# Attention with a gated residual: the last group's gates fetched through ScalarE's queue, its final additions on VectorE

## The chip, the cores and the metric

The kernel runs on one core of one Trainium2 chip. The metric is the device time of one execution in microseconds; medians are given, and each comparison uses runs of the kernel before on the same chip. The experiments ran on three chips, on which the kernel before took 938.11, 937.95 and 938.00 us, so differences of some 0.2 us between experiments are not read. A time is about 2 us longer than the span of the profile (first to last instruction): 938.09 against 936.1 us before the change.

Names: TensorE is PE in the profile, its weight loads PEld, VectorE DVE, ScalarE ACT, GpSimd POOL, SyncE SP. A "q" after the name (POOLq) marks a record of that engine's sequencer.

## The reference, cut to what matters

```python
xn = layernorm(x)                                   # x: 2048 x 640, bf16
q  = xn @ wq                                        # 32 heads of 192
p  = softmax(q @ k[last 512].T * 192**-0.5)
s  = (p @ v[last 512]) @ wo                         # 2048 x 640
g  = silu((sigmoid(xn @ w_gate) * (xn @ w_up)) @ w_down)
return x + s * g
```

## The kernel before

The gate `g` is computed first and stored to a scratch tensor `gB_d` in device memory. Attention then runs over 32 blocks: 8 groups of 4 heads (`g`), each over 4 stretches of 512 rows (`s`). A block computes scores and exponentials, then the products with V; in between it does the output projection of the block before (`stage_wo`), whose four tiles of 128 x 640 are added up over the groups in `acc`. Before the last group, GpSimd prepares each accumulator as `acc * gate + x`. The last group then needs one multiplication (projection times gate) and one addition (plus `acc`) per tile, in `finish`.

```python
    fin = ...tile_pool(name="fin", bufs=2)          # t_sb, xa_sb
    fout = ...tile_pool(name="fout", bufs=4)        # o_sb
    gate_pool = ...tile_pool(name="gate_pool", bufs=TQ + 1)     # TQ = 4

    def load_gate(t):
        gB_sb = gate_pool.tile([P, D], BF16, name="gBa_sb")
        nc.gpsimd.dma_start(gB_sb[:], gB_d[t * P:(t + 1) * P, :])
        return gB_sb

    def prep_last(t):                       # in the last group but one
        ...                                 # loads gate and x of tile t + 1 on nc.gpsimd
        nc.gpsimd.tensor_tensor(acc[t][:], acc[t][:], gB_sb[:], ALU.mult)
        nc.gpsimd.tensor_tensor(acc[t][:], acc[t][:], x_sb[:], ALU.add)

    def finish(ps, gB_sb, t, d0, d1, add):
        t_sb = fin.tile([P, D], F32, name="t_sb")
        o_sb = fout.tile([P, D], BF16, name="o_sb")
        d = slice(d0, d1)
        nc.vector.tensor_tensor(t_sb[:, d], ps, gB_sb[:, d], ALU.mult)
        add.tensor_tensor(o_sb[:, d], t_sb[:, d], acc[t][:, d], ALU.add)
        nc.sync.dma_start(of[t * P:(t + 1) * P, d], o_sb[:, d])

    def stage_wo(n, q):
        ...
        if g == NG - 1:
            for tt in range(t, min(t + 4, NST * TQ)):
                if tt not in gates:
                    gates[tt] = load_gate(tt)
            gB_sb = gates[t]
        if n == last and q == TQ - 1:       # the last tile, in two halves
            ps, h = bank2(), D // 2
            for i in range(2):
                wo_mm(ps[:, i, :], n, q, [(i * h, h)], i * h)
                finish(ps[:, i, 0:h], gB_sb, t, i * h, (i + 1) * h, nc.vector)
            return
        ...
        if g == NG - 1:
            finish(oA[:, 0:D], gB_sb, t, 0, D, nc.gpsimd if n >= last - 1 else nc.vector)
```

The softmax here doesn't subtract the row's maximum and nothing guards it: scores larger than these inputs give would overflow.

Of the kernel before, what the change touches and what calls it, by code (L numbers as in the profile page):

```python
# [9 lines left out]
ALU = mybir.AluOpType  # L10
# [5 lines left out]
def kernel(  # L16
# [13 lines left out]
    nc = tc.nc  # L30
    P = 128
# [4 lines left out]
    S, D = xf.shape  # L36
# [10 lines left out]
    NST = S // 512  # L47
    TQ = 4
# [6 lines left out]
    NG = NPAIR // G  # L55
# [18 lines left out]
    def bank2():  # L74
        b = ring.pop(0)
        ring.append(b)
        return ps_all[:, 2 * b:2 * b + 2, :]

    def flat(ps):
        return ps.rearrange("p b n -> p (b n)")  # L80
# [7 lines left out]
    gB_d = dram.tile([S, D], BF16, name="gB_d")  # L88
# [29 lines left out]
    def load_k(hp, eng):  # L118

        k_sb = k_pool.tile([P, KC * PC, 2, HF], BF16, name="k_sb")  # L120
        for i in range(2):
            hk = (2 * hp + i) // rep
            eng.dma_start(
                k_sb[:, :, i, :],
                A_k_cache[0, hk, Sk - W:Sk, :].rearrange("(p k) (j e) -> p (k j) e", k=KC, j=PC),
            )
        k_of[hp] = k_sb

    def load_v(hp, eng):
        v_t[hp] = []  # L130
        for i in range(2):
            hk = (2 * hp + i) // rep
            vt = v_tiles[(2 * hp + i) % NV]
            eng.dma_start(
                vt[:, :, 0:DH],
                A_v_cache[0, hk, Sk - W:Sk, :].rearrange("(p j) d -> p j d", j=KC),
            )
            v_t[hp].append(vt)

    def load_wq(hp, eng):  # L140


        if hp % G == 0:
            wq_t[hp // G] = wq_pool.tile([P, G * PC // 2, NCD * 2, 2, HF], BF16, name="wqp")
        wqp = wq_t[hp // G]
        for j in range(PC):
            jj = (hp % G) * PC + j
            r = HI if jj % 2 else LO
            for i in range(2):
                d0 = (2 * hp + i) * DH + j * HF  # L150
                eng.dma_start(
                    wqp[r, jj // 2, :, i, :],
                    wq_r[:, :, :, d0:d0 + HF].rearrange("p c h n -> p (c h) n"),
                )

    def turn_k(hp):
        kT = kt_pool.tile([P, KC * PC, P], BF16, name="kT")
        nc.sync.dma_start_transpose(kT[:], k_of[hp][:].rearrange("p k i e -> p (k i e)"))
        kT_t[hp] = kT


    with ExitStack() as bctx:
# [147 lines left out]
        for s in range(NST):  # L310
            hT_sb = hpool.tile([P, NF, 512], BF16, name="hT_sb")
            for f in range(NF):
# [13 lines left out]
                if s + 1 < NST:  # L326
                    t = (s + 1) * TQ
# [7 lines left out]
            for q in range(TQ):  # L335
# [8 lines left out]
                gB_sb = bwork.tile([P, D], BF16, name="gB_sb")  # L344
# [3 lines left out]
                t = s * TQ + q  # L348
# [20 lines left out]
    small = ctx.enter_context(tc.tile_pool(name="small", bufs=8))  # L369
    fin = ctx.enter_context(tc.tile_pool(name="fin", bufs=2))  # L370
    fout = ctx.enter_context(tc.tile_pool(name="fout", bufs=4))
    gate_pool = ctx.enter_context(tc.tile_pool(name="gate_pool", bufs=TQ + 1))

    acc = [acc_pool.tile([P, D], F32, name=f"acc{t}") for t in range(NST * TQ)]
    wo_t = {}

    def load_wo(g, eng):
        wo_g = wo_pool.tile([P, G * PC, D], BF16, name="wo_g")
        eng.dma_start(wo_g[:], wo_r[:, g * G * PC:(g + 1) * G * PC, :])
        wo_t[g] = wo_g  # L380

    def load_ahead(g, s):


        if s < G:
            load_wq(g * G + s, nc.scalar)
            load_k(g * G + s, nc.scalar)
        elif s == G:
            for hp in range(g * G, (g + 1) * G):
                load_v(hp, nc.scalar)  # L390
                turn_k(hp)
        if s == NST - 1:
            load_wo(g, nc.scalar)
# [22 lines left out]
    def stage_s(n, pp, c):  # L416

        g, s = blocks[n]
        kT, qT = kT_t[g * G + pp], qT_t[n]
        if c == 0:  # L420
            E_t[n, pp] = e_pool.tile([P, KC, 2, 512], BF16, name="E")
        ps = bank2()
        for j in range(PC):
            for b, r in enumerate((LO, HI)):
                nc.tensor.matmul(  # L425
                    ps[:, b, :], lhsT=kT[r, c * PC + j, :], rhs=qT[r, pp * PC + j, :],
                    start=(j == 0), stop=(j == PC - 1),
                )
        nc.scalar.activation(E_t[n, pp][:, c, :, :], ps, AF.Exp, scale=scale_qk)  # L429
# [24 lines left out]
            nc.sync.dma_start_transpose(oT[:], o_st[:].rearrange("p q d -> p (q d)"))  # L454
            oT_t[n, pp] = oT

    def load_gate(t):
        gB_sb = gate_pool.tile([P, D], BF16, name="gBa_sb")
        nc.gpsimd.dma_start(gB_sb[:], gB_d[t * P:(t + 1) * P, :])  # L459
        return gB_sb  # L460

    prep_in = {}

    def prep_load(t):
        gB_sb = load_gate(t)
        x_sb = fin.tile([P, D], BF16, name="xa_sb")
        nc.gpsimd.dma_start(x_sb[:], xf[t * P:(t + 1) * P, :])
        prep_in[t] = gB_sb, x_sb

    def prep_last(t):  # L470

        if t == 0:
            prep_load(t)
        if t + 1 < NST * TQ:
            prep_load(t + 1)
        gB_sb, x_sb = prep_in[t]
        nc.gpsimd.tensor_tensor(acc[t][:], acc[t][:], gB_sb[:], ALU.mult)  # L477
        nc.gpsimd.tensor_tensor(acc[t][:], acc[t][:], x_sb[:], ALU.add)

    def wo_mm(oA, n, q, d_ch, base=0):  # L480
        g, s = blocks[n]
        nn = G * PC
        for cc in range(nn):
            pp, j = divmod(cc, PC)
            for d0, dsz in d_ch:
                nc.tensor.matmul(  # L486
                    oA[:, d0 - base:d0 - base + dsz], lhsT=oT_t[n, pp][:, q * PC + j, :],
                    rhs=wo_t[g][:, cc, d0:d0 + dsz],
                    start=(cc == 0), stop=(cc == nn - 1),
                )  # L490

    def finish(ps, gB_sb, t, d0, d1, add):
        t_sb = fin.tile([P, D], F32, name="t_sb")
        o_sb = fout.tile([P, D], BF16, name="o_sb")
        d = slice(d0, d1)
        nc.vector.tensor_tensor(t_sb[:, d], ps, gB_sb[:, d], ALU.mult)  # L496
        add.tensor_tensor(o_sb[:, d], t_sb[:, d], acc[t][:, d], ALU.add)  # L497
        nc.sync.dma_start(of[t * P:(t + 1) * P, d], o_sb[:, d])

    gates = {}  # L500

    def stage_wo(n, q):
        g, s = blocks[n]
        t = s * TQ + q
        if g == NG - 1:

            for tt in range(t, min(t + 4, NST * TQ)):
                if tt not in gates:
                    gates[tt] = load_gate(tt)
            gB_sb = gates[t]  # L510
        if n == last and q == TQ - 1:

            ps, h = bank2(), D // 2
            for i in range(2):
                wo_mm(ps[:, i, :], n, q, [(i * h, h)], i * h)
                finish(ps[:, i, 0:h], gB_sb, t, i * h, (i + 1) * h, nc.vector)
            return
        oA = flat(bank2())
        wo_mm(oA, n, q, d_chunks)
        if g == NG - 1:  # L520
            finish(oA[:, 0:D], gB_sb, t, 0, D, nc.gpsimd if n >= last - 1 else nc.vector)
        elif g == 0:
            nc.vector.tensor_copy(acc[t][:], oA[:, 0:D])
        else:
            nc.vector.tensor_tensor(acc[t][:], oA[:, 0:D], acc[t][:], ALU.add)  # L525
        if g == NG - 2:
            prep_last(t)

    blocks = [(g, s) for g in range(NG) for s in range(NST)]
    last = len(blocks) - 1  # L530
# [4 lines left out]
    for n, (g, s) in enumerate(blocks):  # L535

        todo = [(pp, c) for pp in range(G) for c in range(KC)]
        for k, (pp, c) in enumerate(todo):
            stage_s(n, pp, c)
            if k % 2 == 1 and k // 2 < G * PC // 2 and n < last:  # L540
                stage_q(n + 1, k // 2)
        if g + 1 < NG:
            load_ahead(g + 1, s)

        pv = [(n, pp, i) for pp in range(G) for i in range(2)]
        wo = [(n - 1, q) for q in range(TQ)] if n > 0 else []
        if n < last:
            for k, u in enumerate(pv):
                stage_pv(*u)
                if wo:  # L550
                    stage_wo(*wo[k])
        else:
            for k, u in enumerate(pv):
                stage_pv(*u)
                if k == 1:
                    stage_wo(*wo.pop(0))
            for u in wo:
                stage_wo(*u)
# [31 lines left out]
```

## Time and profile before

| | before |
|---|---|
| time, median of 3 runs | 938.09 us (938.05 to 938.12) |
| span of the profile | 936.1 us |
| TensorE busy | 921.1 us |
| TensorE's last matmul ends | 927.73 us |
| VectorE's last addition ends | 930.87 us |
| SyncE's last wait for an output ends | 932.9 us |
| GpSimd's drain ends | 935.32 us |

The page of the kernel before, cut: busy time and share of the span; busy tenths of the 40 slices of the span; and the queue of DMAs that GpSimd issues (packets, MB, share).

```profile
span 936.1 us, 18189 instructions
...
PE 921.1 (98%) x7945; PEld 539.8 (58%) x8025; DVE 446.7 (48%) x636; ACT 303.8 (32%) x340; POOL 106.8 (11%) x130
...
PE   9999999999999999999999999999999999999996
...
DVE  4443532454444444444444444444444444444654
...
POOL 0070000100000000000000000000000006666005
...
q0 software_dynamic: 4368, 14.03, 5.7%
```

TensorE is busy nine tenths or more of every slice but the last. So what can be gained is in the last slice, where GpSimd (POOL) is at work again after a pause. The timeline of the kernel before, from 914 us on, cut; columns are start, length, engine, line, operation, and in brackets the idle time before it and what ended it:

```profile
916.16 11.57 PE L486 MATMUL ps_all<-wo_g,oT 128*128 128x512 bf16 x82
...
926.65 0.82 DVE L496 TENSOR_TENSOR t_sb<-ps_all,gBa_sb 128x640 f32<-128x640 f32 x1 [1.23 <-POOL o_sb L497]
928.07 1.52 POOL L497 TENSOR_TENSOR o_sb<-t_sb,acc_1587 128x640 bf16<-128x640 f32 x1
928.14 0.49 DVE L496 TENSOR_TENSOR t_sb<-ps_all,gBa_sb 128x320 f32<-128x320 f32 x1 [0.66 <-POOL o_sb L497]
928.66 1.28 DVE L497 TENSOR_TENSOR o_sb<-t_sb,acc_1588 128x320 bf16<-128x320 f32 x1
929.87 0.48 DVE L496 TENSOR_TENSOR t_sb<-ps_all,gBa_sb 128x320 f32<-128x320 f32 x1
930.38 0.49 DVE L497 TENSOR_TENSOR o_sb<-t_sb,acc_1588 128x320 bf16<-128x320 f32 x1
```

TensorE ends at 916.16 + 11.57 = 927.73. GpSimd still adds the last full tile until 929.59, and VectorE's product at 928.14 had to wait 0.66 us for GpSimd, because the product buffer `t_sb` has two copies and GpSimd was still reading one. The half addition at 928.66, beside GpSimd's, took 1.28 us; the other took 0.49. In the table of waits of the same stretch (total us, times, longest us):

```profile
DVE t_sb L496 <- POOL o_sb L497: 2.7, 3, 1.2
```

The records of the kernel's closing line are waits and drains of the engines' sequencers. They are listed with count, shortest/median/longest in ns, and first and last start:

```profile
L585 POOLq DRAIN  x3: 40/102/7804, 927.5 to 935.8; - x3
L585 SPq DRAIN  x3: 7/7/13, 932.9 to 935.6; - x3
```

GpSimd's long drain began at 927.5 and took 7.80 us, so it ended at 935.3. SyncE had waited for every output and began its own drain at 932.9. The closing barrier, which takes 0.78 us, starts only after both: its first record comes at 935.37. So GpSimd alone held the end for some 2.3 us.

### The profile page before, as it was taken

What the parts mean: (1) busy time and instruction counts of PE and PEld (TensorE: products, weight loads), DVE (VectorE), ACT (ScalarE), POOL (GpSimd) and SP (SyncE); (2) the same over time, 40 slices, a digit from 0 to 9 for tenths busy, and PEclk for the clock granted to TensorE, in tenths of its full rate; (3) what the DMA queues carried; (4) which work ended last, traced back from release to release, by engine and by line L of the source; (5) the groups of instructions that cost most, each with busy time, mean ns of one, the idle gap of its engine ahead of it and who ended that gap; (6) DMA issues with size and microseconds to landing.
All of it is one profiled execution on the core that took longest, in us unless ns stands there. A gap on an engine that the chain in (4) does not pass through costs nothing.

```text
span 936.1 us, 18189 instructions
## 1 busy us (share of the span) xinstructions
PE 921.1 (98%) x7945; PEld 539.8 (58%) x8025; DVE 446.7 (48%) x636; ACT 303.8 (32%) x340; POOL 106.8 (11%) x130
## 2 busy tenths in 40 slices
PE   9999999999999999999999999999999999999996
PEld 5545445565555565555556555555555556666664
DVE  4443532454444444444444444444444444444654
ACT  4333322433333333333333333333333333333340
POOL 0070000100000000000000000000000006666005
PEclk9999999999999999999999999999999999999999
DMA  9566030376334523463346324632563348553434
GB/s 281 155 124 118 18 95 15 96 115 100 81 62 65 114 73 53 76 112 77 54 71 121 76 48 70 113 65 70 70 106 69 77 73 162 125 133 98 91 84 119
DMA packets 270144, 87.18 MB, mean 93 GB/s; under 512 B 250288, under 2 KB 266736, under 8 KB 270064
## 3 DMA queue, kind: packets, MB, share of 16 engines
q1 hardware_dynamic: 146864, 47.20, 25.8%
q10 hardware_dynamic: 118832, 24.78, 13.9%
q0 software_dynamic: 4368, 14.03, 5.7%
q8 instruction: 63, 1.03, 0.4%
q14 instruction: 17, 0.14, 0.0%
HBM read 44.70 MB, written 5.24 MB: 53 GB/s over the span
## 4 chain that ended last, share of the span: by engine, by line
PE 96%; issue 1%; POOL 1%; DMA 0%; DVE 0%; ACT 0%; SPq 0%; DVEq 0%; ACTq 0%; POOLq 0%
PE ps_all L409 22%; PE ps_all L486 21%; PE ps_all L441 19%; PE ps_all L425 18%; PE ps_all L319 10%; PE ps_all L339 6%; PE ps_all L260 1%; DMA x_sb_138<-in_A_x_dram 0%; POOL o_sb L497 0%; ACT E L429 0%; DVE t_sb L496 0%; POOL gBa_sb L459 0%; DVE stats L222 0%; SPq L175 0%; ACT xnT_93 L275 0%
## 5 line engine op out<-in xcount | busy, mean ns | idle before, releaser
L429 ACT ACTIVATE E<-ps_all 128x1024 bf16<-128x1024 f32 x256 | 247.8, 1022 | 496.2 <-PE ps_all L425 443.7
L486 PE MATMUL ps_all<-wo_g,oT 128*128 128x128 bf16 (+2 forms) x1473 | 224.9, 295 | 3.3
L414 DVE CAST qT<-ps_all 128x1024 bf16<-128x1024 f32 x96 | 117.5, 1224 | 226.4 <-PE ps_all L409 226.4
L425 PE MATMUL ps_all<-qT,kT 64*128 64x512 bf16 x1536 | 186.7, 376 | 0.0
L441 PEld LDWEIGHTS <-E 128*128 128x128 bf16 x2048 | 171.0, 98 | 24.4 <-issue 13.6
L486 PEld LDWEIGHTS <-oT 128*128 128x128 bf16 x1536 | 121.4, 97 | 76.2
L409 PEld LDWEIGHTS <-wqp 64*128 64x128 bf16 x1920 | 93.4, 94 | 113.8 <-issue 0.3
L425 PEld LDWEIGHTS <-kT 64*128 64x128 bf16 x1536 | 72.3, 94 | 91.8 <-issue 8.4
L448 DVE TENSOR_TENSOR o_st<-ps_all,rden 128x768 bf16<-128x768 f32 x128 | 122.5, 957 | 4.8 <-DVE rden L447 0.5
L447 DVE RECIPROCAL rden<-ps_all 128x4 f32<-128x4 f32 x128 | 23.3, 182 | 98.9 <-PE ps_all L441 98.7
L477 POOL TENSOR_TENSOR acc_1573<-acc_1573,gBa_sb 128x640 f32<-128x640 f32 x1 | 1.4, 1397 | 603.4 <-DVE acc_1573 L525 603.4
L325 DVE TENSOR_TENSOR hT_sb<-ps_all,sig_sb 128x512 bf16<-128x512 f32 x48 | 33.1, 691 | 50.9 <-PE ps_all L319 40.9
L409 PE MATMUL ps_all<-xnT_94,wqp 64*128 64x512 bf16 x240 | 55.7, 376 | 0.0
L409 PE MATMUL ps_all<-xnT_95,wqp 64*128 64x512 bf16 x240 | 55.7, 376 | 0.0
L409 PE MATMUL ps_all<-xnT_96,wqp 64*128 64x512 bf16 x240 | 55.7, 376 | 0.0
L409 PE MATMUL ps_all<-xnS_90,wqp 64*128 64x512 bf16 x240 | 55.6, 376 | 0.0
L409 PE MATMUL ps_all<-xnS_91,wqp 64*128 64x512 bf16 x240 | 55.6, 376 | 0.0
L409 PE MATMUL ps_all<-xnS_92,wqp 64*128 64x512 bf16 x240 | 55.6, 376 | 0.0
L409 PE MATMUL ps_all<-xnT_93,wqp 64*128 64x512 bf16 x240 | 55.4, 376 | 0.0
L409 PE MATMUL ps_all<-xnS_89,wqp 64*128 64x512 bf16 x240 | 55.3, 376 | 0.0
L339 PE MATMUL ps_all<-wd_sb,hT_sb 128*128 128x128 bf16 (+1 forms) x377 | 52.4, 298 | 0.4
L324 ACT ACTIVATE sig_sb<-ps_all 128x512 bf16<-128x512 f32 x48 | 28.6, 597 | 56.6 <-PE ps_all L319 56.2
(159 smaller groups left out, 696.5 us busy)
## 6 DMA issues: line engine op xcount, KB each, us to landing
wqp<-in_A_wq_dram ACTq DMA_DIRECT2D x84, 80.0 KB, 3.0
wo_g<-in_A_wo_dram ACTq DMA_DIRECT2D x7, 960.0 KB, 5.1
k_sb<-in_A_k_cache_dram ACTq DMA_DIRECT2D x28, 192.0 KB, 4.6
gBa_sb<-gB_d POOLq DMA_DIRECT2D x32, 160.0 KB, 2.9
gB_d<-gB_sb POOLq DMA_DIRECT2D x16, 160.0 KB, 2.5
xa_sb<-in_A_x_dram POOLq DMA_DIRECT2D x16, 160.0 KB, 3.2
out_dram<-o_sb SPq DMA_DIRECT2D x15, 160.0 KB, 2.2
wd_sb<-in_B_w_down_dram SPq DMA_DIRECT2D x1, 1920.0 KB, 11.8
```

The source lines that it names most:

```text
L319: nc.tensor.matmul(gu[:, i, :], lhsT=w[:, c, f * P:(f + 1) * P], rhs=xnT[s][:, c, :], start=(c == 0), stop=(c == NCD - 1),)
L324: nc.scalar.activation(sig_sb[:], gu[:, 0, :], AF.Sigmoid)
L325: nc.vector.tensor_tensor(hT_sb[:, f, :], gu[:, 1, :], sig_sb[:], ALU.mult)
L339: nc.tensor.matmul(oB_ps[:, d0:d0 + dsz], lhsT=hT_sb[:, f, q * P:(q + 1) * P], rhs=wd_sb[:, f, d0:d0 + dsz], start=(f == 0), stop=(f == NF ...
L409: nc.tensor.matmul(ps[:, b, :], lhsT=wq_t[g][r, u, 2 * c + h].rearrange("p i e -> p (i e)"), rhs=x[s][r, c, :], start=(c == 0 and h == 0), ...
L414: nc.vector.tensor_copy(qT_t[n][:, 2 * u:2 * u + 2, :], ps)
L425: nc.tensor.matmul(ps[:, b, :], lhsT=kT[r, c * PC + j, :], rhs=qT[r, pp * PC + j, :], start=(j == 0), stop=(j == PC - 1),)
L429: nc.scalar.activation(E_t[n, pp][:, c, :, :], ps, AF.Exp, scale=scale_qk)
L441: nc.tensor.matmul(o_ps[:, q // 2, q % 2, 0:DH + 1], lhsT=E[:, c, i, q * P:(q + 1) * P], rhs=vt[:, c, 0:DH + 1], start=(c == 0), stop=(c = ...
L447: nc.vector.reciprocal(rden[:], o_ps[:, :, :, DH:DH + 1])
L448: nc.vector.tensor_tensor(o_st[:, :, i * DH:(i + 1) * DH].rearrange("p (b i) d -> p b i d", b=2), o_ps[:, :, :, 0:DH], rden[:].to_broadcas ...
L486: nc.tensor.matmul(oA[:, d0 - base:d0 - base + dsz], lhsT=oT_t[n, pp][:, q * PC + j, :], rhs=wo_t[g][:, cc, d0:d0 + dsz], start=(cc == 0), ...
```

## The change

Its intent: have no GpSimd work near the end. The gates of the last group are loaded through ScalarE's queue, behind the exponentials of the block in which they are used (in the last block, with those of the last block's own tiles); there are six gate buffers instead of five; and all additions in `finish` are VectorE's.

```diff
-    gate_pool = ...tile_pool(name="gate_pool", bufs=TQ + 1)
+    gate_pool = ...tile_pool(name="gate_pool", bufs=TQ + 2)
-    def load_gate(t):
+    def load_gate(t, eng):
-        nc.gpsimd.dma_start(gB_sb[:], gB_d[t * P:(t + 1) * P, :])
+        eng.dma_start(gB_sb[:], gB_d[t * P:(t + 1) * P, :])
     def prep_load(t):
-        gB_sb = load_gate(t)
+        gB_sb = load_gate(t, nc.gpsimd)
-    def finish(ps, gB_sb, t, d0, d1, add):
+    def finish(ps, gB_sb, t, d0, d1):
-        add.tensor_tensor(o_sb[:, d], t_sb[:, d], acc[t][:, d], ALU.add)
+        nc.vector.tensor_tensor(o_sb[:, d], t_sb[:, d], acc[t][:, d], ALU.add)
     def stage_wo(n, q):
-        if g == NG - 1:
-            for tt in range(t, min(t + 4, NST * TQ)):
-                if tt not in gates:
-                    gates[tt] = load_gate(tt)
-            gB_sb = gates[t]
+        gB_sb = gates.get(t)
 ... (the calls of finish lose their last argument)
     for n, (g, s) in enumerate(blocks):
         ... (scores, exponentials, load_ahead)
+        for m in (n - 1, n) if n == last else (n - 1,):
+            if n > 0 and blocks[m][0] == NG - 1:
+                for t in range(blocks[m][1] * TQ, blocks[m][1] * TQ + TQ):
+                    gates[t] = load_gate(t, nc.scalar)
```

More of the change, by code (lines that the diff above doesn't have):

```diff
@@ L371 @@
     fout = ctx.enter_context(tc.tile_pool(name="fout", bufs=4))
-    gate_pool = ctx.enter_context(tc.tile_pool(name="gate_pool", bufs=TQ + 1))
+    gate_pool = ctx.enter_context(tc.tile_pool(name="gate_pool", bufs=TQ + 2))
     acc = [acc_pool.tile([P, D], F32, name=f"acc{t}") for t in range(NST * TQ)]
@@ L515, in stage_wo @@
                 wo_mm(ps[:, i, :], n, q, [(i * h, h)], i * h)
-                finish(ps[:, i, 0:h], gB_sb, t, i * h, (i + 1) * h, nc.vector)
+                finish(ps[:, i, 0:h], gB_sb, t, i * h, (i + 1) * h)
             return
@@ L520, in stage_wo @@
         if g == NG - 1:
-            finish(oA[:, 0:D], gB_sb, t, 0, D, nc.gpsimd if n >= last - 1 else nc.vector)
+            finish(oA[:, 0:D], gB_sb, t, 0, D)
         elif g == 0:
```

## The prediction

> **What bounds the kernel now.** TensorE. The page gives it 921.1 us busy of a 936.1 us span (98%), the granted clock is full, and the table of waits shows TensorE waiting only some 2 us in all, all of it in the first stage. So only the tail can be shortened. By the timeline TensorE's last matmul ends at about 927.7 us, and 8.4 us pass until the span ends.
>
> The tail:
> - The last four output tiles wait on the slower adder. GpSimd's final additions take 1.53 to 1.55 us each, plus 0.55 us for each gate load that it issues between them, while TensorE finishes a tile each 1.63 us. VectorE waits for GpSimd three times (2.7 us in all).
> - One of the last half additions on VectorE takes 1.28 us instead of 0.49, beside a GpSimd addition. The Trainium skill ("SBUF — State Buffer", Who interferes with whom) says a VectorE instruction with two SBUF inputs contends with a GpSimd instruction that reads SBUF; the trace agrees.
> - VectorE ends at 930.87, the last output lands at 932.45, SyncE's own waits end at 933.0. But GpSimd's final drain runs on to 935.33, 5.7 us after its last addition (929.59), and only then does the closing barrier (0.78 us) follow. So some 2.3 us is waiting for GpSimd alone.
>
> **What the change removes, adds and moves.** It takes seven additions (10.8 us) and sixteen gate loads off GpSimd, whose last work then is the preparation of the accumulators, ending at 861.4. VectorE gets the seven additions at 0.83 us each. ScalarE gets sixteen issues, estimated at 0.4 to 0.65 us each from its present loads, after the last exponential of a block, in time that it has free (11.6 us idle between blocks).
>
> **Critical path.**
> 1. VectorE tail. A product and an addition take about 1.67 us per tile together (start to start at 898 to 900 us), against TensorE's 1.63. Six full tiles from 917.99, then the two halves (four operations, about 0.5 us each), end at about 929.95 instead of 930.87: 0.9 us less.
> 2. GpSimd's drain falls out of the end: the output lands at 931.5, SyncE is done at 932.0, and with 0.78 us of barrier the span ends near 932.8: another 2.3 us less.
> 3. Gates may be late. In the last block the issue can start while the seventh exponential runs (its neighbours' loads do so), about 910.6; with 2.3 to 2.9 us to land that is 912.9 to 913.5, against a need at 913.69. Any lateness delays the output transposition that the last block's projection needs; there is about 0.4 us of slack. I expect no stall, or a few tenths.
>
> Sum: 3.2 us off, so 938.09 becomes 934.9. Range 933.8 to 936.9. Chances: faster by over 2% 0.005, within 2% 0.99, slower by over 2% 0.005.
>
> **What would show it right or wrong.** Right: TensorE's busy time unchanged; no GpSimd record after 862 us except the closing barrier, its drain ended long before; SyncE's last wait for the output directly before the barrier; both last half additions at 0.49 us; VectorE's last addition ends near 930. Wrong: the first product of each of the last three blocks waiting for a gate; gaps in TensorE near 921 us; the drain still ending last.
>
> **What would make it wrong.** The drain's 5.7 us could belong to something that the change leaves (the output's landing, say), then only 0.9 us is won. Six gate loads in one burst could slow the transpositions of the last block, and TensorE would stall by 0.5 to 1.5 us.

## The result and the profile after

The kernel after takes 934.88 us (934.65 to 935.11, 4 runs) against 938.07 us (937.87 to 938.12, 4 runs): 3.2 us less. Ratios are the mean time of one kernel's fast runs over that of the other's of the same rounds, so not quite the ratio of the medians: 0.9966, with a 95% interval of 0.9949 to 0.9984. That is inside 2%, and clear of no change.

| | before | after |
|---|---|---|
| TensorE's last matmul ends | 927.73 | 927.67 |
| VectorE's last addition ends | 930.87 | 930.18 |
| SyncE's drains done | 933.0 | 932.3 |
| GpSimd's drain ends | 935.32 | 865.83 |
| span | 936.1 | 933.1 |
| span after TensorE's end | 8.4 | 5.4 |

The last row is the useful one. It leaves out the first stage, whose length varies by some tenths of a microsecond from run to run, and it says that all of the gain lies in the tail. The page of the kernel after:

```profile
span 933.1 us, 18277 instructions
...
PE 924.7 (99%) x8025; PEld 539.4 (58%) x8025; DVE 451.2 (48%) x643; ACT 303.8 (33%) x340; POOL 87.9 (9%) x107
...
PE   8999999999999999999999999999999999999997
...
DVE  4443532454444444444444444444444444444657
...
POOL 0070000100000000000000000000000006665000
...
q0 software_dynamic: 3600, 11.41, 4.8%
```

GpSimd's slices are empty at the end, and its queue moves 2.6 MB less (16 gate loads of 160 KB). TensorE's busy time looks 3.6 us longer, but 80 of its 8025 matmul records are missing from the trace of before; the instructions are the same, and TensorE waits for nothing after the first stage in either trace. The tail, to be held against the one of before:

```profile
916.10 11.57 PE L486 MATMUL ps_all<-wo_g,oT 128*128 128x512 bf16 x84
...
927.10 0.83 DVE L497 TENSOR_TENSOR o_sb<-t_sb,acc_1587 128x640 bf16<-128x640 f32 x1
927.84 0.48 DVE L496 TENSOR_TENSOR t_sb<-ps_all,gBa_sb 128x320 f32<-128x320 f32 x1
928.77 0.49 DVE L497 TENSOR_TENSOR o_sb<-t_sb,acc_1588 128x320 bf16<-128x320 f32 x1 [0.44 <-issue]
929.17 0.48 DVE L496 TENSOR_TENSOR t_sb<-ps_all,gBa_sb 128x320 f32<-128x320 f32 x1
929.69 0.49 DVE L497 TENSOR_TENSOR o_sb<-t_sb,acc_1588 128x320 bf16<-128x320 f32 x1
```

Both half additions take 0.49 us, and no product waits for GpSimd. But the first half addition stands 0.44 us idle for nothing that the profile shows ("issue"). The waits of this stretch say the same:

```profile
DVE t_sb L496 <- PE ps_all L486: 0.8, 2, 0.4
DVE o_sb L497 <- issue: 0.4, 1, 0.4
```

The closing records:

```profile
L584 POOLq DRAIN  x3: 40/102/5861, 860.0 to 932.8; - x3
L584 SPq DRAIN  x3: 7/7/13, 932.2 to 932.6; - x3
```

GpSimd's drain now begins at 860.0, takes 5.86 us and is over at 865.8. SyncE's drain at 932.2 is the last before the barrier.

The gates come in time. These are ScalarE's issues in the last block, and the first product that needs one of them (each row is from the timeline of its engine):

```profile
908.98 0.81 ACTq L459 DMA_DIRECT2D gBa_sb<-gB_d  x2
...
909.89 1.57 ACTq L459 DMA_DIRECT2D gBa_sb<-gB_d  x2
```

```profile
913.64 0.82 DVE L496 TENSOR_TENSOR t_sb<-ps_all,gBa_sb 128x640 f32<-128x640 f32 x1 [0.44 <-PE ps_all L486]
```

The first gate was issued 4.7 us before its product, and that product waited for TensorE, not for a load.

### The profile page after: what moved, and what is told of

It is laid out like the page before. It is cut to its first block, busy times and chain, and to the rows that moved or that the text cites. A ratio compares the mean times of both kernels' runs of the same rounds, so it can differ in the third digit from the quotient of the medians.

```text
span 933.1 us, 18277 instructions
## 1 busy us (share of the span) xinstructions
PE 924.7 (99%) x8025; PEld 539.4 (58%) x8025; DVE 451.2 (48%) x643; ACT 303.8 (33%) x340; POOL 87.9 (9%) x107
## 3 DMA queue, kind: packets, MB, share of 16 engines
q8 instruction: 63, 1.03, 0.5%
## 5 line engine op out<-in xcount | busy, mean ns | idle before, releaser
L486 PE MATMUL ps_all<-wo_g,oT 128*128 128x512 bf16 (+2 forms) x1536 | 228.2, 299 | 0.0
L339 PE MATMUL ps_all<-wd_sb,hT_sb 128*128 128x512 bf16 (+1 forms) x384 | 52.8, 299 | 0.0
```

The lines of the kernel that those rows point to most:

```text
L339: nc.tensor.matmul(oB_ps[:, d0:d0 + dsz], lhsT=hT_sb[:, f, q * P:(q + 1) * P], rhs=wd_sb[:, f, d0:d0 + dsz], start=(f == 0), stop=(f == NF ...
L486: nc.tensor.matmul(oA[:, d0 - base:d0 - base + dsz], lhsT=oT_t[n, pp][:, q * PC + j, :], rhs=wo_t[g][:, cc, d0:d0 + dsz], start=(cc == 0), ...
```

## The experiments

Theory: the change gains because GpSimd's closing drain leaves the end (2.3 us), and because VectorE no longer waits for GpSimd or beside it (0.7 us). Rivals: that moving the gate loads is what matters; that the late additions themselves do, whatever the drain; that the gap of 0.44 us in VectorE is a wait for an output buffer. Twelve kernels ran. "Tail of the span" below is the span less the end of TensorE's last matmul.

### The additions alone

The kernel before with one edit:

```diff
-            finish(oA[:, 0:D], gB_sb, t, 0, D, nc.gpsimd if n >= last - 1 else nc.vector)
+            finish(oA[:, 0:D], gB_sb, t, 0, D, nc.vector)
```

> The kernel before, with only the last additions moved to VectorE; the gate loads stay on GpSimd. Theory (the gain is GpSimd's closing drain leaving the end, plus VectorE's shorter tail; the drain runs some 4.4 to 5.8 us from GpSimd's last work, whatever that is): the last gate load is issued near 920.5, so the drain ends near 925 to 926.5, before SyncE is done at 932.3; nearly the whole gain is there, 934.9 +- 0.4 us. Rival (moving the gate loads off GpSimd is what gains): the time stays near 938, or the drain ends after 932.

Measured: 934.93 us (934.65 to 935.02), ratio to before 0.9967 (0.9954 to 0.9979); tail of the span 5.4 us, as in the kernel after. The closing records:

```profile
L585 POOLq DRAIN  x3: 40/93/6413, 920.8 to 932.9; - x3
L585 SPq DRAIN  x3: 7/7/7, 932.3 to 932.6; - x3
```

The drain's record begins at 920.8, while the last gate load is being issued (until 921.3; in these traces such a record starts before the last instruction is done), and ends at 927.2. It is hidden. So the additions alone give the whole gain, and the gate loads need not have moved.

### The gates alone

The kernel after, with `nc.gpsimd if n >= last - 1 else nc.vector` back in the call of `finish`.

> The kernel after, with the last additions back on GpSimd; only the gate loads are on ScalarE. GpSimd then needs 1.53 us per tile and keeps up with TensorE's 1.63, so its last addition ends near 928.6. If the drain's tail follows GpSimd's last work of any kind, it ends at 928.6 + 4.4 to 5.8 = 933.0 to 934.4 and the span at 933.8 to 935.2 (time 935.8 to 937.2): little gain. If the tail belongs to late software DMA alone, the drain ends just after 928.6 and the time is 934.5 or less: as good as the kernel after.

Measured: 935.62 us (935.53 to 936.03), ratio 0.9976 (0.9963 to 0.9988); tail of the span 6.15 us. The timeline, cut, and the closing records:

```profile
918.72 9.74 POOL L497 TENSOR_TENSOR o_sb<-t_sb,acc 128x640 bf16<-128x640 f32 x6 [2.76 <-DVE t_sb L496]
...
927.39 1.41 DVE L497 TENSOR_TENSOR o_sb<-t_sb,acc 128x320 bf16<-128x320 f32 x1
```

```profile
L584 POOLq DRAIN  x3: 40/93/5994, 926.9 to 933.4; - x3
L584 SPq DRAIN  x3: 7/7/7, 931.8 to 933.1; - x3
```

GpSimd keeps up without the loads between its additions and ends at 928.46 instead of 929.59. Its drain ends at 932.9, later than SyncE's (931.8), and still holds the end. This was slightly better than the range expected, and the reason is instructive: the drain ran 4.42 us past GpSimd's last work, not 5.73 as before. So the two halves of the change do not add up: either alone brings GpSimd's drain forward, the additions by enough and the loads by 2.4 us. And a DMA issued late by GpSimd is not needed for a slow drain: one came here after additions alone.

### One late addition

The kernel after, with only the last full tile's addition on GpSimd (`nc.gpsimd if t == NST * TQ - 2 else nc.vector`).

> The kernel after with one addition alone, that of the last full tile, back on GpSimd, ending near 928.7. Theory (one late GpSimd instruction is enough to put the drain at the end): the drain ends at 933.1 to 934.5, the last record before the closing barrier, and the time is 0.8 to 2.2 us above the kernel after, 935.7 to 937.1. Rival (the drain's tail grows with the amount of late GpSimd work, or comes from late software DMA): the drain ends before 932.3 and the time is within 0.5 us of the kernel after.

Measured: 935.67 us (935.61 to 935.79), ratio 0.9975 (0.9963 to 0.9988); tail of the span 6.1 us. The one GpSimd instruction of the tail, and the closing records:

```profile
927.10 1.53 POOL L497 TENSOR_TENSOR o_sb<-t_sb,acc 128x640 bf16<-128x640 f32 x1 [65.71 <-DVE t_sb L496]
```

```profile
L584 POOLq DRAIN  x3: 40/93/5994, 927.1 to 933.6; - x3
L584 SPq DRAIN  x3: 7/7/7, 932.0 to 933.3; - x3
```

VectorE ended earlier than in the kernel after (929.9 against 930.2), yet the run is 0.8 us slower (0.7 us slower than the additions-alone run of the same chip), because the drain ends at 927.06 + 5.99 = 933.05. One GpSimd instruction of 1.53 us is enough. The theory holds and its rival falls.

### What sets the length of the drain

The drain ran on after GpSimd's last work by 5.73 us in the kernel before and in the additions-alone run by 5.85, but by 4.4 us in the other runs, at 861 us as well as at 928. What differs is how many DMAs GpSimd had issued in the whole program: 85 against 69. Two runs move more of them away.

First, the run with one late addition, with the 32 loads that prepare the accumulators on SyncE's queue (37 DMAs stay on GpSimd):

```diff
-        gB_sb = load_gate(t, nc.gpsimd)
+        gB_sb = load_gate(t, nc.sync)
-        nc.gpsimd.dma_start(x_sb[:], xf[t * P:(t + 1) * P, :])
+        nc.sync.dma_start(x_sb[:], xf[t * P:(t + 1) * P, :])
```

> The run with one late addition on GpSimd, with the 32 loads that prepare the accumulators moved from GpSimd's queue to SyncE's, so GpSimd issues 37 DMAs instead of 69. So far the drain's tail after GpSimd's last work was 5.7 to 5.8 us with 85 DMAs issued by GpSimd in the whole program, and 4.4 to 4.5 us with 69, whether the last work was an addition or a load and whether it came at 861 or 928 us. Theory (the tail grows with the DMAs that GpSimd has issued in the whole program): 1.7 us (straight line) to 2.4 us (in proportion), the drain ends before 931.2, SyncE ends the run and the time is 934.3 to 934.8. Rival (the tail belongs to a drain that comes right after late work, a fixed 4.4 us here): the drain ends near 933.05 again and the time is 935.7.

Measured: 934.70 us (934.37 to 934.95), ratio 0.9965 (0.9953 to 0.9978); tail of the span 5.1 us. The drain ends at 930.56, before SyncE is done, as the theory has it.

```profile
L584 POOLq DRAIN  x3: 40/93/3382, 927.2 to 932.6; - x3
L584 SPq DRAIN  x3: 7/7/7, 932.1 to 932.4; - x3
```

Second, the run with the gates alone, with the two edits above and all other DMAs of GpSimd (`gB_d`, the first K, V, wq and wo) on SyncE as well, so that GpSimd issues none:

> The run with the gates on ScalarE and the additions on GpSimd, with every other DMA of GpSimd on SyncE, so GpSimd issues none. Theory (tail grows with GpSimd's DMAs): the tail is below 0.5 us, the drain ends before 929.2 in spite of the late additions, VectorE ends near 929.7, SyncE is done at 931.8 and the time is 934.2 to 934.6, a little below the kernel after. Rival (fixed tail after late GpSimd work): drain ends near 932.9, time 935.6 as before.

Measured: 934.34 us (934.17 to 934.82), ratio 0.9963 (0.9949 to 0.9976); tail of the span 4.7 us.

```profile
L584 POOLq DRAIN  x3: 34/77/1637, 926.8 to 931.9; - x3
L584 SPq DRAIN  x3: 7/7/7, 931.4 to 931.7; - x3
```

Here GpSimd does seven late additions, as in the kernel before, and its drain ends at 926.84 + 1.64 = 928.48, 0.07 us after the last of them. The rival, a drain that is slow after any late work, falls. Variants of the kernel after tested the straight line that these points suggest. The first cut each preparation load into two halves by columns (101 DMAs, the same bytes):

> The kernel after with each of the 32 preparation loads cut into two halves by columns: 101 DMAs of GpSimd instead of 69, the same bytes. The drain starts near 860 and hides, but its length can be read. If the tail goes with the number of DMAs (or descriptors), it is 6.5 to 7.1 us after GpSimd's last addition; if with bytes, 4.4 us as now.

The tail was 0.91 us, which neither reading had foreseen. So two more: each load of x issued twice (85 DMAs), and every preparation load issued twice, whole (101 DMAs):

> The kernel after with each of the 16 loads of x on GpSimd's queue issued twice: 85 DMAs of GpSimd. The drain hides, its length can be read. The straight line through 37, 69 and 85 DMAs gives a tail of 5.7 to 5.8 us; the run with 101 smaller ones broke it with 0.9 us.

> The kernel after with all 32 preparation loads on GpSimd's queue issued twice, whole: 101 DMAs of GpSimd. If the tail falls back once a certain number of DMAs has been passed, it is near 0.9 us as with the 101 halves; if the halves were what made it short, it is near 7.1 us.

They gave 5.73 and 0.91 us. (The last run took 976 us: GpSimd waited for each load before repeating it into the same buffer, its preparation ended only at 934.3, VectorE's products waited 42 us in all for their gates, and TensorE 30 us for VectorE's products. That says nothing of the change.) All points together, worked out from the start and length of the drain's record and the end of GpSimd's last instruction:

| DMAs issued by GpSimd | run | last work | drain past its end, us |
|---|---|---|---|
| 0 | none from GpSimd | additions, 928.4 | 0.07 |
| 37 | preparation on SyncE | one addition, 928.8 | 1.81 |
| 69 | after | preparation, 861.4 | 4.42 |
| 69 | gates alone | additions, 928.5 | 4.42 |
| 69 | one late addition | one addition, 928.6 | 4.42 |
| 85 | before | additions, 929.6 | 5.73 |
| 85 | additions alone | gate load, 921.3 | 5.85 |
| 85 | x loaded twice | preparation, 887.1 | 5.73 |
| 101 | preparation in halves | preparation, 863.3 | 0.91 |
| 101 | preparation twice | preparation, 934.3 | 0.91 |

The length follows the number of DMAs issued before it in the program (or of their packets), not when or what kind of work came last: at 69 and at 85 both were varied and it stayed within 0.12 us. It rises by about 0.08 us per DMA from 37 to 85 (1.3 us for 16, 2.6 us for 32), and falls back once some number between 85 and 101 has been passed. Bytes are excluded: the two runs with 101 moved 11.4 and 16.7 MB. Packets cannot be told from DMAs: each DMA by which the runs from 37 to 101 differ made 48 packets, whole or halved. Nor was the missing time spent in one long issue earlier: in every run with DMAs on GpSimd the longest issue took 1.03 to 1.04 us. What the drain does in that time, and why it falls back, no run here shows; that stays open.

### The gap of 0.44 us: an output buffer?

VectorE's stream holds a wait for an output buffer just before the late half addition, so a missing buffer was the first guess. The kernel after with one more output buffer (five) and one gate buffer less (five):

> The kernel after with five output buffers instead of four and five gate buffers instead of six. Theory (the first half addition waited 0.44 us for an output buffer whose store had not landed, a wait that the change brought): VectorE's last addition starts 0.4 us earlier and the time falls from 934.9 to about 934.45. Rival (that gap is something else): no change, 934.9.

Measured: 935.08 us (934.91 to 935.34), ratio 0.9969 (0.9956 to 0.9983); tail of the span 5.4 us, and the gap is there unchanged. The guess is refuted. (The trace of the kernel after agrees: the store that this wait names, issued at 923.00, had landed by 925.2.)

### The gap: a fixed place in VectorE's stream?

Four more tiny memsets on VectorE at the start of the kernel after:

```diff
-    nc.vector.memset(eps_t[:], eps)
+    for _ in range(5):
+        nc.vector.memset(eps_t[:], eps)
```

> The kernel after with four more tiny memsets on VectorE at the start. In the kernel after, VectorE's first half addition stands 0.44 us with nothing that the profile shows, and five output buffers did not change that. If the gap sits at a fixed place in VectorE's stream of instructions (something about fetching them), it moves to an earlier instruction or goes; if it belongs to that addition itself, it stays there at about 0.4 us.

The timeline of that run, cut (lines are one further down than in the kernel after, so L498 is the addition):

```profile
927.24 0.82 DVE L498 TENSOR_TENSOR o_sb<-t_sb,acc 128x640 bf16<-128x640 f32 x1 [0.44 <-issue]
...
928.56 0.49 DVE L498 TENSOR_TENSOR o_sb<-t_sb,acc 128x320 bf16<-128x320 f32 x1
```

The gap moved to the addition of the last full tile, four records earlier in VectorE's queue; the half addition at 928.56 has none. Counting VectorE's records in the traces, semaphore waits included, the instruction with the gap is the 960th in the kernel after, here, and in the runs with the additions alone, with five buffers, with halved loads and with x or everything loaded twice. In the kernel before VectorE's stream ends with its 955th record: the change lengthened it past that place. Next, 44 memsets, spread over early tiles where VectorE has time, to put the place where VectorE idles:

```diff
         gB_sb = gates.get(t)
+        if 16 <= g * NST * TQ + t < 16 + 44:
+            nc.vector.memset(pad_t[:], 0.0)
```

> The kernel after with 44 tiny memsets on VectorE, one per output tile in early groups where VectorE has time. Four memsets moved the unexplained gap of 0.4 us to the instruction four earlier in VectorE's queue; 44 should put it where VectorE idles, near 905 to 910 us. Theory (the gap sits at a fixed place in VectorE's stream, and costs the end only where it falls): no gap in the last tiles, VectorE's last addition starts 0.4 us earlier, time 934.45 instead of 934.88. Rival (hidden anyway, something else holds the end): 934.9.

Measured: 934.35 us (934.17 to 934.68), ratio 0.9962 (0.9949 to 0.9974); tail of the span 5.05 us instead of 5.4. The halves of the last tile (product, addition, product, addition; lines are one further down):

```profile
927.52 0.48 DVE L497 TENSOR_TENSOR t_sb<-ps_all,gBa_sb 128x320 f32<-128x320 f32 x1
928.09 0.49 DVE L498 TENSOR_TENSOR o_sb<-t_sb,acc 128x320 bf16<-128x320 f32 x1
928.50 0.48 DVE L497 TENSOR_TENSOR t_sb<-ps_all,gBa_sb 128x320 f32<-128x320 f32 x1
929.02 0.49 DVE L498 TENSOR_TENSOR o_sb<-t_sb,acc 128x320 bf16<-128x320 f32 x1
```

The gap is gone, and the tail is shorter by 0.35 us. So the gap belongs to a place in the instruction stream, not to any data. Trainium skill, "Runtime: NRT & Kernel Launch", Instruction fetch mechanics: instructions are refilled in blocks of 256, and crossing a block's end is "mostly hidden". A fetch that was not hidden would fit; no run was made to test it.

The traces show more of it than the experiments set out to test. In the kernel after, the wait in front of the 960th record ended at 928.37, and the addition began 0.40 us later; the median of 220 such steps is 0.04 us. The extra 0.35 us agrees with what the 44 memsets won back. The same 0.40 us stands at the 832nd record of the kernel after, at the 704th (another instruction) with four memsets ahead, and at the 576th and 832nd in the run without any DMA from GpSimd; past the first 130 us of these three traces no other such step takes over 0.15 us. All these places are multiples of 128 records apart. The DMA queue that the profile calls "instruction" (q14) fits that: eight of its packets of 8192 bytes in the kernel after come when VectorE has begun its 65th, 191st, 318th, 448th, 578th, 705th, 832nd and 962nd record (the last two at 843.56 and 929.54 us), and with 44 memsets the last of them comes at 906.25 us, with 959 begun. So the gap sits at the edge of a block of 128 of VectorE's instructions. But the packet starts 0.7 to 0.8 us after the late instruction has begun, so what VectorE does in the gap is not shown, and a wait for a fetch stays argued.

### A faster version

The run without any DMA from GpSimd lost time at one place: VectorE's second product began only at 928.68. Two things held it until then: its buffer came free when GpSimd's last addition ended (928.41), and VectorE's first half addition, 1.41 us long beside that one, ended at 928.76 (two operations in a row overlap a little). With both products of the last tile in one buffer, and ahead of both additions:

```diff
+            t_sb = fin.tile([P, D], F32, name="t_sb")
+            ds = [slice(0, h), slice(h, D)]
             for i in range(2):
                 wo_mm(ps[:, i, :], n, q, [(i * h, h)], i * h)
-                finish(ps[:, i, 0:h], gB_sb, t, i * h, (i + 1) * h, nc.vector)
+                nc.vector.tensor_tensor(t_sb[:, ds[i]], ps[:, i, 0:h], gB_sb[:, ds[i]], ALU.mult)
+            for d in ds:
+                o_sb = fout.tile([P, D], BF16, name="o_sb")
+                nc.vector.tensor_tensor(o_sb[:, d], t_sb[:, d], acc[t][:, d], ALU.add)
+                nc.sync.dma_start(of[t * P:(t + 1) * P, d], o_sb[:, d])
```

> The run without any DMA from GpSimd, with the last tile's two products before its two additions and both products in one buffer. There the second product waited for GpSimd's last addition (it stood until 928.7) only because it took that addition's buffer. Expected: second product near 927.9, both half additions right after GpSimd's addition ends at 928.4, VectorE done near 929.45 instead of 929.7, time 934.1 instead of 934.34. Rival (the order does not matter, the store's landing decides): 934.3.

Measured: 934.09 us (933.61 to 934.21), ratio 0.9958 (0.9944 to 0.9971); tail of the span 4.4 us. It has the lowest median: 0.8 us under the kernel after, 3.9 us under the kernel before of the same rounds (938.0). Against the run that it was made from (934.34) the times overlap and the chips differ; there the traces decide, with VectorE done at 929.17 instead of 929.69. The edit does two things at once, the order and the shared buffer, and no run parts them. Its tail:

```profile
920.37 8.05 POOL L497 TENSOR_TENSOR o_sb<-t_sb,acc 128x640 bf16<-128x640 f32 x5 [0.15 <-DVE t_sb L496]
...
926.83 0.49 DVE L513 TENSOR_TENSOR t_sb<-ps_all,gBa_sb 128x320 f32<-128x320 f32 x1
927.56 0.49 DVE L513 TENSOR_TENSOR t_sb<-ps_all,gBa_sb 128x320 f32<-128x320 f32 x1 [0.23 <-PE ps_all L486]
927.97 1.21 DVE L516 TENSOR_TENSOR o_sb<-t_sb,acc 128x320 bf16<-128x320 f32 x2
```

VectorE ends at 929.2, 1.7 us after TensorE, where the kernel after needs 2.5. Some 0.35 us of that is the gap: with additions back on GpSimd, VectorE's stream has 951 records and never reaches the 960th.

## Why the prediction was right

934.9 us was predicted, in a range of 933.8 to 936.9; 934.88 was measured. The mechanism was right, but agreement to 0.02 us is luck: the runs of the kernel after span 0.46 us, the two profiles add up to 0.69 + 2.32 = 3.0 us where 3.2 was predicted, and two terms were mis-sized, as said below. Point by point:

- **TensorE bounds the kernel and only the tail can change: right.** The span after TensorE's end fell from 8.4 to 5.4 us, and TensorE's end moved by 0.06 us, which is within the drift of the first stage.
- **GpSimd's drain leaves the end, 2.3 us: right, and the step carried most of the gain.** The drain had ended 2.32 us after SyncE was done. The run with one late addition brings it back to the end at a cost of 0.8 us, and the additions-alone run shows that GpSimd's last work may come as late as 921.3, 11 us before SyncE is done. What the prediction did not know is that the drain's length goes with the DMAs (or packets) that GpSimd issued.
- **VectorE's tail, 0.9 us: the mechanism was right, the size off.** VectorE ended 0.69 us earlier. The pace (1.65 us per tile, 918.85 to 920.50 us) and the half additions at 0.49 us came as predicted; the term missed the gap of 0.44 us at the 960th record, which VectorE's stream reaches only since it got the seven additions and their waits (967 records instead of 955). Without it the tail was 0.35 us shorter. Part of the miss was made up by operations that overlap a little at their ends.
- **The contention of the half addition with GpSimd: agrees.** Trainium skill, "SBUF — State Buffer", Who interferes with whom: a VectorE instruction with two SBUF inputs contends with a GpSimd instruction that reads SBUF. The half addition has two; it took 1.28 us beside GpSimd's addition before, 0.49 us after; in the gates-alone run (927.39) 1.41 us again.
- **Gates in time: right, by two errors that cancelled.** The first was issued at 908.98, earlier than the 910.6 estimated, but the loads of this burst took 2.8 to 3.6 us to land, not 2.3 to 2.9. The first landed at 912.6, 1.1 us before its product; issued at 910.6, with 3.6 us to land, it would have come 0.5 us late. No product waited for a load. The issues took 0.33 to 0.45 us each, but for one of 1.09, so mostly at or below the estimate's low end of 0.4.
- **No stall of TensorE from the burst of gate loads: right.** The last block's two output transpositions took 5.0 and 3.9 us to land instead of 3.7 each, inside the slack: TensorE's end moved by 0.06 us, forward.

The prediction treated the whole change as one. The runs show that its second half, the gate loads, was not needed for the gain once the additions had moved.

## What to carry to other kernels

Read the closing records of a kernel whose tail matters: an engine's drain can end the run long after its last useful instruction, and then one small instruction on that engine near the end costs more than it saves. Move the last work off it some microseconds early, or take away what makes its drain long; here that was the number of DMAs issued from GpSimd's queue, or of their packets, and with none of them even late additions on GpSimd were free of it. When an engine stands idle for nothing that the profile shows, test whether the gap follows the data or the position in the instruction stream before buying buffers for it.

## What the Trainium skill lacked or had wrong

- "VectorE: DVE Perf Modes", The DRAIN you can't avoid, speaks of the runtime's own drains at the beginning and end of a kernel, some 12 ns each and constant on all five engines, and not of those that carry the program's own closing line. In the kernel before, SyncE's of these took 7 to 13 ns, but GpSimd's longest took 7.80 us and ended 5.73 us after its last work.
- No page says that GpSimd's closing drain goes with the DMAs that were issued from its queue, or with their packets ("DMA: Bandwidth & Descriptors", SWDGE vs HWDGE vs iDMA, would be the place): 0.07 us past the last work with none, 1.81 with 37, 4.4 with 69, 5.7 to 5.9 with 85, and 0.91 with 101.
- "Runtime: NRT & Kernel Launch", Instruction fetch mechanics, has blocks of 256 instructions (16 KiB) and calls the cost of a block's end mostly hidden. For TensorE the traces agree on the size (63 packets of 16384 bytes for the 16100 records of the kernel after). VectorE's packets were of 8192 bytes, one each 128 records, and an operation at such an edge came 0.40 us after its wait instead of 0.04; at the 960th record 0.35 us of that lengthened the kernel. Whether the fetch itself is what VectorE waits for is open.
- "DMA: Bandwidth & Descriptors", Issuing engine by pattern, calls DMAs from SyncE's and ScalarE's queues generally faster than those from GpSimd's. These traces don't decide it: the last group's 16 gate loads of 160 KB landed after 3.0 us (median) through ScalarE, and after 2.8 us through GpSimd in the kernel before, while the other 16 gate loads, through GpSimd, took 3.6 us in the kernel after. The traffic beside them differed.
